# Linear attention and a maxout layer on one core: keys turned into one span over two PSUM banks, the 1e-9 of the queries as a sum of two, another order of the work

## The chip, the cores and the metric

The kernel runs on one core of a Trainium2 chip. The time is that of one execution on the device, in microseconds (us). The engines are PE (matrix products and transposes), DVE and ACT (element by element, from SBUF or PSUM), POOL (element by element, SBUF only) and the DMA queues, which the instruction streams of SP and ACT feed. Each engine works through its own list of instructions in order and waits on semaphores for the others.

## The reference

Attention without a softmax over pairs: queries are normalised over their 64 features, keys over the 576 positions, and the products of keys and values (64 by 64 for a head) are applied to the queries. The result goes through a layer of three products, the largest of which is kept, and an output product. All in float32, for 8 batches of 8 heads.

```python
q_s = np.exp(q - np.max(q, axis=-1, keepdims=True))
q_s = q_s / (np.sum(q_s, axis=-1, keepdims=True) + 1e-09)
k_s = np.exp(k - np.max(k, axis=2, keepdims=True))
k_s = k_s / (np.sum(k_s, axis=2, keepdims=True) + 1e-09)
kv = np.einsum('bhsd,bhse->bhde', k_s, v)
x = np.einsum('bhsd,bhde->bhse', q_s, kv)          # to 4608 rows of 512
h = np.maximum(np.maximum(x @ w1, x @ w2), x @ w3)  # 768 wide
out = h @ w_out
```

## The kernel before

Float32 products run as three products of a high and a low part in a faster type; each weight and each activation is split into such parts. The heads are taken in 32 pairs (a batch has four). The first two batches are "turned" pairs: `k_turned` (L623) transposes their keys on PE, so that positions lie along the free dimension, takes the maximum there on DVE, the exponential and its sum on ACT, and transposes back; `k_steps` (L695) goes on to the product with the values (L708), the reciprocal of the sum and the block matrix `bdf` (L720). The other 24 pairs are "plain": the maximum over positions is taken by POOL across partitions (L680), and two pairs at a time form a `Quad`, whose step on PE holds the products of keys and values of the next quad (L865) and the application to the queries of this one (L914). `q_steps` (L723) normalises the queries of a pair: maximum (L732 or L762), then, for pairs in `Q_BY_ACT`, one activation for each row with the maximum as bias and the sum as accumulator (L749, L767), else a subtraction, an exponential and a sum (L754 or L773, L778, L780); then the 1e-9 is added (L782), the reciprocal taken (L783) and multiplied in (L786).

The weights come in twelve slices (`Slice`, loaded at L489), are rounded and split on ACT, DVE and POOL (L505 to L548), and feed the gates: chunk by chunk for three chunks (`Chunk.gate`, L958, in groups of three products over one of four parts of x; L970 takes the maximum, L997 is the output product), and two chunks at a time with seven products instead of eight after that (`Duo.gates`, L1134, `Duo.second`, L1245).

The order of all this is not written down. Each part is a generator that yields steps, with an engine, a cost, what it waits for and which room (a PSUM bank, a buffer) it takes; `Streams.run` (L235) plays them against clocks of the engines and issues the instructions in the order that this gives. Ranks come from the tables at the head of the file, `LATE`, `Q_OFF`, `LOAD_OFF` and others. Where the planner sees PE idle, `fill` (L264) puts products of the identity with itself there (L457, from `filler`); ahead of the first step there are always eight, of a zeroed matrix (`IDLE_FIRST`). `FIRST_LOADS` gives the order of the first transfers (k, q, v: a pair's main rows; K, V: rest rows; w: a weight slice), and the first `FIRST_ON_ACT` of them may go to the queue of SP or of ACT. Eight semaphores are shared in turn by the transfers: a transfer that takes one again waits until the one that had it has landed.

PSUM has eight banks of 512 columns. Seven, `banks`, are handed out by the planner; the eighth is cut into four quarters (`small`, L452) for the small results: the last 64 columns of the turned keys (L635), their way back (L658), and the products of keys and values.

Of the kernel before, what the change touches and what calls it, by code (L numbers as in the profile page):

```python
# [36 lines left out]
SLICE = 225.18  # L37
LATE = (-245.5, -738.3, 170.7, 1076.1, 129.3, 336.8, 110.3, -591.5, 283.8, 139.9, -217.0, -419.4, 227.8, 729.6, 1717.3, 928.9, -4.1, 2054.6, 2040.9, 1513.5, 1739.1, 1826.7, 1494.9, 1573.0)
SUMS = (-733.7, -414.9, 85.3, 292.8, 1712.0, -374.3, 235.7, 406.3, 80.5)
KEPT = (107.0, -865.1, -45.2, -717.4, -1581.6, -900.1, -1174.0, -1366.7, -1728.2)  # L40
KEPT_RANK = 130.16
SLICE_OFF = (-340.2, -56.5, -907.2, -1080.6, -281.4, 597.2, 906.3, 417.9, 733.8, 516.7, 231.2, -111.0)
Q_OFF = (64.6, 1741.9, -395.6, -554.3, -297.6, 259.5, 483.6, 696.1, 858.9, 107.2, -846.4, 810.3, -294.1, 578.6, -714.3, -872.6, -323.0, 47.8, 428.2, 70.6, -145.8, 345.1, -642.9, 1226.8, 1104.8, -656.7, 635.3, 97.3, -96.9, 574.5, -54.6, -455.7)
LOAD_OFF = (-278.4, -22.2, -809.9, 466.9, 228.2, -747.5, -668.2, 212.2, -287.6, 241.8, -718.1, -298.3, 18.0, 918.3, -241.3, 259.7, -542.2, 133.3, -214.9, 1068.4, 1359.0, -703.2, 91.3, 840.3, 658.3, 313.8, 517.4, -68.2, 151.4, 996.4, 422.5, -604.7)
LOADS_AHEAD = 170.42

AT = (-454.7, 519.6, 1348.2, -133.6, 1086.9, 233.6, 436.9, 1101.5)
STEP = (-534.1, 491.2)
SLICES_AT = -84.14
SLICE_STEP = 134.98  # L50
SLICE_HI = -258.29
SLICE_LO = 126.09
GATES_AT = -85.68
FIRST_LOADS = 'kqKkwqvqvKqkvVwvVk'
FIRST_ON_ACT = 9
LEFT_AT = -132.76
# [10 lines left out]
SPARE_X, SPARE_KV, SPARE_RING, SPARE_LOAD, SPARE_KM = 2.52, 4.6, 0.0, 1.33, 1.58  # L67
# [245 lines left out]
def linear_attention_then_maxout_ffn(  # L313
# [48 lines left out]
    ps = ctx.enter_context(tc.tile_pool(name="ps", bufs=1, space=PSUM))  # L362
# [26 lines left out]
    bds = []  # L389
    early = early_stack.enter_context(tc.tile_pool(name="early", bufs=1))  # L390
# [6 lines left out]
    nc.vector.memset(ones, 1.0)  # L397
    count = early.tile([P, P], F32, name="count")
# [30 lines left out]
    def banks_of_heads(key):  # L429
        return (4, 5, 6) if key[-1] < NP * (PLAIN + 2) else range(7)  # L430
# [4 lines left out]
    for d in range((B + 1 - PLAIN) // 2):  # L435
# [3 lines left out]
        {"pf": banks_of_gates, "pa": banks_of_heads, "ring": RING, "ws": 1, "sums": 1, "halves": 2, "ps": 4, "keT": ROOM_KET, "hp": NJ, "tmp": N_TMP, "ke": 2, "qe": ROOM_QE, "qf": ROOM_QF, "qt": 2, "tb": N_TB, "qT": N_QT},  # L439
# [11 lines left out]
    quarters = ps.tile([P, 4, P], F32, name="ps")  # L451
    small = (quarters[:, i % 4, :] for i in itertools.count())  # L452
# [110 lines left out]
    class Pair:  # L563
# [131 lines left out]
        def k_steps(self):  # L695
# [18 lines left out]
            nc.vector.tensor_scalar(  # L714
                out=rk, in0=self.ks[:, 0:1], scalar1=self.ks[:, 1:2], scalar2=1e-9, op0=ALU.add, op1=ALU.add
            )
            nc.vector.reciprocal(out=rk, in_=rk)
# [845 lines left out]
```

## Time and profile before

| | |
|---|---|
| median of three runs | 659.4 us (653.69, 659.4, 660.97) |
| profiled execution | 657.82 us, its span 656.0 us |
| PE busy, of the span | 98% (clock 0.997 of full) |
| DVE, ACT, POOL busy | 69%, 43%, 9% |
| moved by DMA | 140.65 MB |

The page cuts the span into 40 slices of 16.4 us, each digit a tenth:

```profile
PE   9899999999999999899999999999999999999997
DVE  7998777679988988999989792144548614454521
ACT  5867485266563755743534454111113421112132
DMA  8899896368989899989999773466660536663012
```

PE has work nearly all the time; DVE and DMA are close to full over the first 23 slices (375 us), in which the attention is computed beside the gates, and half idle behind it. A busy PE includes the filler products.

### The profile page before, as it was taken

The numbers are of one execution on the slowest core, as the hardware profiler recorded it, in microseconds if no ns is written. First come the engines' busy times: TensorE is split into PE (matmuls) and PEld (weight loads), VectorE is DVE, ScalarE is ACT, GpSimd is POOL, SyncE is SP. The second block draws the span as 40 slices with busy tenths as digits, with TensorE's granted clock in tenths as the row PEclk, the third lists the DMA queues.
The fourth block names the chain that finished last, engine by engine and source line by source line (L and its number), as shares of the span: only waits on it lengthen the run. The fifth ranks groups of instructions, "written<-read, shape, count | busy, mean of one in ns | idle before, by whom it ended". The sixth has DMA issues, their size and how long they took to land.

```text
span 656.0 us, 10034 instructions
## 1 busy us (share of the span) xinstructions
PE 642.1 (98%) x3596; PEld 520.7 (79%) x3596; DVE 452.4 (69%) x785; ACT 281.4 (43%) x722; POOL 57.1 (9%) x71
## 2 busy tenths in 40 slices
PE   9899999999999999899999999999999999999997
PEld 8677778888777787677777887888888888888885
DVE  7998777679988988999989792144548614454521
ACT  5867485266563755743534454111113421112132
POOL 1322333201000010000110000000000000000000
PEclk9998999999999999999999999999999999999999
DMA  8899896368989899989999773466660536663012
GB/s 262 257 322 334 257 353 198 116 213 265 280 261 325 271 250 332 254 275 264 286 286 281 207 221 134 144 206 176 196 194 17 192 113 200 190 199 118 0 65 64
DMA packets 116770, 140.65 MB, mean 214 GB/s; under 512 B 53616, under 2 KB 75888, under 8 KB 115568
## 3 DMA queue, kind: packets, MB, share of 16 engines
q1 hardware_dynamic: 111552, 134.02, 66.8%
q10 hardware_dynamic: 5168, 6.00, 3.2%
q8 instruction: 28, 0.46, 0.3%
q14 instruction: 22, 0.18, 0.1%
HBM read 102.24 MB, written 37.75 MB: 213 GB/s over the span
## 4 chain that ended last, share of the span: by engine, by line
PE 84%; DMA 8%; DVE 2%; ACT 1%; SPq 1%; issue 0%; DVEq 0%; ACTq 0%
PE bank L1134 37%; PE bank L958 17%; PE bank L1245 15%; PE bank L997 7%; DMA kt<-in_k_dram 2%; DMA turned<-tb 2%; PE ps L865 2%; PE bank L457 1%; PE bank L914 1%; PE bank L831 1%; DMA wst<-in_moe_w_dram 1%; DMA qT<-turned 1%; DMA vt<-in_v_dram 1%; PE ps L708 1%; DMA qt<-in_q_dram 1%; PE bank L815 0%
## 5 line engine op out<-in xcount | busy, mean ns | idle before, releaser
L1134 PE MATMUL bank<-gw 128*128 128x512 f32 x1134 | 260.2, 390 | 0.5 <-DVE m L1202 0.5
L1134 PEld LDWEIGHTS bank<-gw 128*128 128x128 f32 x1134 | 212.3, 188 | 48.4 <-issue 1.6
L958 PE MATMUL bank<-gw 128*128 128x512 f32 x432 | 104.8, 399 | 0.0
L958 PEld LDWEIGHTS bank<-gw 128*128 128x128 f32 x432 | 81.1, 190 | 20.7 <-issue 3.9
L1245 PE MATMUL bank<-oh,halves 128*128 128x512 f32 x288 | 88.7, 389 | 0.0
L1245 PEld LDWEIGHTS bank<-oh,halves 128*128 128x128 f32 x288 | 54.1, 188 | 11.2
L1245 PE MATMUL bank<-ol,halves 128*128 128x512 f32 x144 | 56.3, 391 | 0.0
L958 PE MATMUL bank<-x,gw 128*128 128x512 f32 x216 | 49.9, 390 | 0.0
L958 PEld LDWEIGHTS bank<-x,gw 128*128 128x128 f32 x216 | 40.4, 188 | 9.2 <-issue 0.8
L1223 DVE TENSOR_TENSOR halves<-hf,halves 128x768 fp32r<-128x768 f32 (+2 forms) x30 | 23.6, 794 | 34.3 <-ACT halves L1221 34.2
L767 ACT ACTIVATE qt<-qt,qm 128x64 f32<-128x64 f32 x126 | 42.3, 339 | 11.6 <-DVE qm L762 9.8
L997 PE MATMUL bank<-oh,h 128*128 128x512 f32 x144 | 44.4, 389 | 0.0
L680 POOL PARTITION_ALL_REDUCE kma<-kh x24 | 18.3, 762 | 204.9 <-DVE kh L677 80.2
L1264 ACT COPY m<-bank 128x512 f32<-128x512 f32 x23 | 13.5, 589 | 52.4 <-PE bank L1245 52.4
L1196 ACT COPY m<-bank 128x512 f32<-128x512 f32 x18 | 10.6, 588 | 57.9 <-PE bank L1134 55.2
L1191 ACT COPY m<-bank 128x512 f32<-128x512 f32 x18 | 10.6, 587 | 54.8 <-PE bank L1134 50.0
L1245 PEld LDWEIGHTS bank<-ol,halves 128*128 128x128 f32 x144 | 27.0, 188 | 7.2 <-ACT left L923 0.8
L970 DVE TENSOR_TENSOR m<-bank,m 128x512 f32<-128x512 f32 x36 | 24.7, 685 | 11.2 <-PE bank L958 8.6
L997 PEld LDWEIGHTS bank<-oh,h 128*128 128x128 f32 x144 | 27.0, 188 | 5.6
L791 DVE STREAM_TRANSPOSE tb<-qt 128x576 f32<-128x576 f32 x24 | 30.3, 1269 | 0.2
L1198 DVE TENSOR_TENSOR m<-bank,m 128x512 f32<-128x512 f32 x18 | 12.4, 690 | 25.6 <-PE bank L1134 25.2
L997 PE MATMUL bank<-ol,h 128*128 128x512 f32 x72 | 28.3, 393 | 0.0
(162 smaller groups left out, 867.1 us busy)
## 6 DMA issues: line engine op xcount, KB each, us to landing
gw<-scratch SPq DMA_DIRECT2D x75, 512.0 KB, 3.7
gw<-scratch SPq DMA_DIRECT2D x39, 256.0 KB, 3.8
wst<-in_moe_w_dram SPq DMA_DIRECT2D x9, 1024.0 KB, 8.0
scratch<-bench SPq DMA_DIRECT2D x9, 1024.0 KB, 6.0
out_dram<-m SPq DMA_DIRECT2D x32, 256.0 KB, 2.2
vt<-in_v_dram SPq DMA_DIRECT2D x56, 128.0 KB, 5.2
scratch<-gw SPq DMA_DIRECT2D x27, 256.0 KB, 3.5
qt<-in_q_dram SPq DMA_DIRECT2D x24, 288.0 KB, 4.4
```

The source lines that it names most:

```text
L680: nc.gpsimd.partition_all_reduce(kma, kmv.rearrange("p h d -> p (h d)"), P, bass_isa.ReduceOp.max)
L767: nc.scalar.activation(out=rows3[:, i, :], in_=rows3[:, i, :], func=AF.Exp, bias=qm[:, i : i + 1], accum_out=qs[:, i : i + 1],)
L791: nc.vector.transpose(out=tb.rearrange("p e (c s) -> p s e c", s=QS), in_=self.qt.rearrange("p s (c e) -> p s e c", e=2))
L865: nc.tensor.matmul(out=kv[u][r, :NV], lhsT=p.ke[:, s, u, :], rhs=p.vt[:, u, s, :], start=(s == 0), stop=(s == 4))
L958: nc.tensor.matmul(out=ps, lhsT=l[:, cc], rhs=r, start=(cc == 0 and t == 0), stop=(cc == NC - 1 and t == 2))
L970: nc.vector.tensor_max(out=m, in0=self.m.pop((j, i)), in1=m)
L997: nc.tensor.matmul(out=po, lhsT=l, rhs=r[:, j, :], start=(j == 0 and i == 0), stop=(j == NJ - 1 and i == 2))
L1134: nc.tensor.matmul(out=po, lhsT=w[:, a, cc], rhs=x[:, b, cc], start=(first and cc == 0 and t == 0), stop=(cc == 1 and t == 2), skip_group_ ...
L1198: nc.vector.tensor_sub(out=ma, in0=po("w"), in1=ma)
L1223: nc.vector.tensor_sub(out=hl, in0=src, in1=hh.bitcast(F32))
L1245: nc.tensor.matmul(out=po, lhsT=l, rhs=r[:, j, :], start=(j == 0 and i == 0), stop=(end and i == 2))
L1264: nc.scalar.copy(out=o, in_=po)
```

## The change

The seventh bank and the eighth become one tile, `span`, of 1024 columns. The turned keys of a pair take its first 576 columns, always there, so that one maximum and one activation read all of them, across the border of the two banks; the other three quarters of the eighth bank stay for the small results. The sum of a pair's keys is then one number, and the 1e-9 is added from a column that holds it. For the queries a tile of sums has two places for each row: one is set to 1e-9 once, the other takes the sum, and a reduction over the two replaces the addition. The tables that order the work are all new (a line or two are shown), the first chunk's gates have four banks instead of five, and 24 pairs are in `Q_BY_ACT` instead of 18.

```diff
-FIRST_LOADS = 'kqKkwqvqvKqkvVwvVk'
-FIRST_ON_ACT = 9
+FIRST_LOADS = 'vvqwKkkvkVqqKVwqvk'
+FIRST_ON_ACT = 7
-Q_BY_ACT = (1, 2, 6, 7, 8, 9, 10, 11, 12, 13, 14, 17, 18, 20, 22, 25, 27, 31)
+Q_BY_ACT = (1, 3, 4, 5, 6, 9, 10, 11, 12, 13, 17, 18, 19, 20, 21, 23, 24, 25, 26, 27, 28, 29, 30, 31)
-FIRST_BANKS = 5
+FIRST_BANKS = 4
...
-    banks = [pf.tile([P, CH], F32, name=f"bank{i}") for i in range(7)]
+    banks = [pf.tile([P, CH], F32, name=f"bank{i}") for i in range(6)]
+    span = pf.tile([P, 2 * CH], F32, name="span")
+    banks.append(span[:, :CH])
...
+    sum_all = att.tile([P, 4, QS, 2], F32, name="qs", bufs=1)
+    sums_of = (sum_all[:, i % 4] for i in itertools.count())
...
+    nc.vector.memset(least, 1e-9)
+    nc.gpsimd.memset(sum_all, 1e-9)
...
-            yield Step("V", dve_reduce(CH) + dve_reduce(LEFT) + 0.13)
-            km = att.tile([P, 2], F32, name="km2", bufs=4)
-            nc.vector.tensor_reduce(out=km[:, 0:1], in_=kT, op=ALU.max, axis=AX.X, negate=True)
-            nc.vector.tensor_reduce(out=km[:, 1:2], in_=kTl[:, :LEFT], op=ALU.max, axis=AX.X, negate=True)
-            nc.vector.tensor_scalar(
-                out=km[:, 0:1], in0=km[:, 0:1], scalar1=km[:, 1:2], scalar2=None, op0=ALU.min
-            )
-            yield Step("A", act(CH) + act(LEFT) + 0.2, free=rooms)
+            yield Step("V", 0.75)
+            km = att.tile([P, 1], F32, name="km2", bufs=4)
+            nc.vector.tensor_reduce(out=km, in_=kT, op=ALU.max, axis=AX.X, negate=True)
+            yield Step("A", 0.98, free=rooms)
...
-            nc.scalar.activation(out=keT[:, :CH], in_=kT, func=AF.Exp, bias=km[:, 0:1], accum_out=ks[:, 0:1])
-            nc.scalar.activation(
-                out=keT[:, CH:], in_=kTl[:, :LEFT], func=AF.Exp, bias=km[:, 0:1], accum_out=ks[:, 1:2]
-            )
+            nc.scalar.activation(out=keT, in_=kT, func=AF.Exp, bias=km, accum_out=ks)
...
             yield Step("V", 0.34)
-            nc.vector.tensor_scalar_add(out=qs, in0=qs, scalar1=1e-9)
-            nc.vector.reciprocal(out=qs, in_=qs)
+            nc.vector.tensor_reduce(out=qr, in_=sums, op=ALU.add, axis=AX.X)
+            nc.vector.reciprocal(out=qr, in_=qr)
```

ACT's list at the start of the program, before (k, q, v are the first batch's tiles, wst a weight slice; in brackets the semaphores waited for, DMAHW those of transfers):

```order
L1387 DMA k_98<-in_k_dram 128x4x64
L1394 DMA k_98<-in_k_dram 64x2x64
L1387 DMA k_98<-in_k_dram 128x4x64
L1390 DMA q_99<-in_q_dram 128x2x256
L1398 ACT_TABLE_LOAD
L1398 ACTIVATE warm<-ones 128x1 [waits DVE_49]
L778 ACTIVATE qe<-qe 128x512 [waits DVE_49]
```

and now:

```order
L1392 DMA v_98<-in_v_dram 128x2x256
L497 DMA wst<-in_moe_w_dram 128x4x512
L1400 ACT_TABLE_LOAD
L1400 ACTIVATE warm<-ones 128x1 [waits DVE_49]
L1389 DMA k_96<-in_k_dram 128x4x64 [waits DMAHW2_49]
L1389 DMA k_96<-in_k_dram 128x4x64 [waits DMAHW4_49]
L778 ACTIVATE qe<-qe 128x512 [waits DVE_49]
L542 ACTIVATE wst<-wst 128x1024
```

The key loads have moved behind values and the first weight slice, and the first of the two waits on DMAHW2. DVE's list shows whose semaphore that is: its first operation on the weight slice waits on the same one.

```order
L782 TENSOR_REDUCE qr_142<-qs 128x8 [waits DVE_49]
L783 RECIPROCAL qr_142<-qr_142 128x8 [waits DVE_49]
L515 TENSOR_SCALAR left<-wst 128x1024 [waits DMAHW2_49]
L786 TENSOR_TENSOR qe<-qe,qr_142 128x512 [waits DVE_49]
L517 TENSOR_SCALAR left<-left 128x1024 [waits DVE_49]
```

The addition of the 1e-9 has become the reduction in the first of these rows. PE's list at the start, before:

```order
L457 MATMUL bank_81<-bdf_108 128x128 x8
L630 MATMUL bank_85<-ident,k_98 128x128 x4
L457 MATMUL bank_81<-ident 128x128 x7
L636 MATMUL ps<-ident,k_98 128x64
L457 MATMUL bank_81<-ident 128x128 x12
L657 MATMUL bank_86<-ident,keT 128x128 x4
L659 MATMUL ps<-ident,keT 64x128
L815 MATMUL bank_87<-ident,qe 128x128 x4
L457 MATMUL bank_81<-ident 128x128 x13
```

and now:

```order
L465 MATMUL bank_78<-bdf_106 128x128 x8
L638 MATMUL span<-ident,k_96 128x128 x4
L465 MATMUL bank_78<-ident 128x128 x7
L644 MATMUL span<-ident,k_96 128x64
L815 MATMUL bank_82<-ident,qe 128x128 x4
L465 MATMUL bank_78<-ident 128x128 x9
L658 MATMUL bank_83<-ident,keT 128x128 x4
L660 MATMUL span<-ident,keT 64x128
L465 MATMUL bank_78<-ident 128x128 x4
```

The fillers (L457, now L465) are fewer behind the first key's transposes, and the queries' transposes stand ahead of the way back of the keys. In all the list holds 74 filler products where it held 93: 66 for 71 up to the first long run of gates, 8 for 22 behind it. Behind that run PE's list was

```order
L457 MATMUL bank_83<-ident 128x128 x2
L708 MATMUL ps<-vt_94,ke 64x64 x10
L457 MATMUL bank_83<-ident 128x128 x4
L958 MATMUL bank_83<-gw 128x512 x12
L657 MATMUL bank_85<-ident,keT 128x128 x4
L659 MATMUL ps<-ident,keT 64x128
L815 MATMUL bank_87<-ident,qe 128x128 x4
```

and is now

```order
L658 MATMUL span<-ident,keT 128x128 x4
L660 MATMUL span<-ident,keT 64x128
L815 MATMUL bank_82<-ident,qe 128x128 x4
L465 MATMUL bank_81<-ident 128x128 x4
L638 MATMUL span<-ident,kt_88 128x128 x4
L644 MATMUL span<-ident,kt_88 128x64
L958 MATMUL bank_81<-gw 128x512 x3
```

One pair's turned keys are left behind the run, where there were three. Of the later batches, the groups of key and value products (L865) stood behind 378, 441, 516, 615, 675 and 741 of the gate and output products and stand now behind 393, 447, 510, 561, 657 and 720. On ACT 45 more single-row activations of queries stand in the later batches; POOL does three of the multiplications by the reciprocal (L786), and DVE copies six of the tiles of keys back from PSUM (L666, now L667) where it copied two.

More of the change, by code (lines that the diff above doesn't have):

```diff
@@ L35 @@
 EAGER = 0.3
[L37 to L42, printed above, removed]
@@ L429, in banks_of_heads @@
     def banks_of_heads(key):
+        if key[0] == "kT":
+            return (6,)
         return (4, 5, 6) if key[-1] < NP * (PLAIN + 2) else range(7)
@@ L438, in linear_attention_then_maxout_ffn @@
     st = Streams(
-        {"pf": banks_of_gates, "pa": banks_of_heads, "ring": RING, "ws": 1, "sums": 1, "halves": 2, "ps": 4, "keT": ROOM_KET, "hp": NJ, "tmp": N_TMP, "ke": 2, "qe": ROOM_QE, "qf": ROOM_QF, "qt": 2, "tb": N_TB, "qT": N_QT},
+        {"pf": banks_of_gates, "pa": banks_of_heads, "ring": RING, "ws": 1, "sums": 1, "halves": 2, "ps": 3, "kTl": 1, "keT": ROOM_KET, "hp": NJ, "tmp": N_TMP, "ke": 2, "qe": ROOM_QE, "qf": ROOM_QF, "qt": 2, "tb": N_TB, "qT": N_QT},
         {
@@ L449, in linear_attention_then_maxout_ffn @@
     late_pools, turn_pools, raws = [], [], []
-    quarters = ps.tile([P, 4, P], F32, name="ps")
-    small = (quarters[:, i % 4, :] for i in itertools.count())
+    quarters = span[:, CH:].rearrange("p (i n) -> p i n", i=4)
+    small = (quarters[:, 1 + i % 3, :] for i in itertools.count())
     def filler(i, n, t):
@@ L625, in k_turned @@
             n, kt = self.n, self.kt
-            rooms = [("pa", ("kT", n)), ("ps", ("kTl", n))]
+            rooms = [("pa", ("kT", n)), ("kTl", n)]
             yield Step("T", 0.74, [("k", n)], take=rooms + [("keT", n)], gives=("ksub", n))
-            kT = banks[st.bank("pa", ("kT", n))]
+            kT = span[:, :S]
             for s in range(4):
@@ L713, in k_steps @@
             rk = att.tile([P, 1], F32, name="rk", bufs=4)
-            nc.vector.tensor_scalar(
-                out=rk, in0=self.ks[:, 0:1], scalar1=self.ks[:, 1:2], scalar2=1e-9, op0=ALU.add, op1=ALU.add
-            )
+            nc.vector.tensor_scalar(out=rk, in0=self.ks, scalar1=least, scalar2=None, op0=ALU.add)
             nc.vector.reciprocal(out=rk, in_=rk)
@@ L742, in q_steps @@
                 rows3 = qe.rearrange("p s h d -> p (s h) d")
-                sums = qs.rearrange("p (s h) -> p s h", h=2)
                 if by_act:
@@ L1280, in left_queries @@
             nc.sync.dma_start(out=rows[r], in_=left_rows(q, b, slice(0, H)))
-        qm, qs = (att.tile([P, n], F32, name=name, bufs=4) for name in ("qm8", "qs8"))
+        qm = att.tile([P, n], F32, name="qm8", bufs=3)
+        qr = att.tile([P, n], F32, name="qr8", bufs=2)
         yield Step("V", dve_reduce(CH))
@@ L1288, in left_queries @@
         yield Step("V", dve_reduce(CH))
-        nc.vector.tensor_reduce(out=qs, in_=rows, op=ALU.add, axis=AX.X)
+        sums = next(sums_of)[:, :n]
+        nc.vector.tensor_reduce(out=sums[:, :, 0], in_=rows, op=ALU.add, axis=AX.X)
         yield Step("V", 0.34)
-        nc.vector.tensor_scalar_add(out=qs, in0=qs, scalar1=1e-9)
-        nc.vector.reciprocal(out=qs, in_=qs)
+        nc.vector.tensor_reduce(out=qr, in_=sums, op=ALU.add, axis=AX.X)
+        nc.vector.reciprocal(out=qr, in_=qr)
         yield Step("V", dve(CH), port="V")
-        nc.vector.tensor_tensor(out=rows, in0=rows, in1=qs.unsqueeze(2).broadcast_to([P, n, D]), op=ALU.mult)
+        nc.vector.tensor_tensor(out=rows, in0=rows, in1=qr.unsqueeze(2).broadcast_to([P, n, D]), op=ALU.mult)
         yield Step("T", 0.7, take=[("pa", ("lq", n - 1))], free=[("tmp", "ql")])
```

52 lines of the change are left out of this document (30 added, 22 removed).

## The prediction

> **What bounds the kernel now.** I read the page's busy shares first, then PE by stages, then what ended PE's waits, then the first 62 us of PE, DVE, ACT and the DMA queues in order of time.
>
> ```profile
> span 656.0 us, 10034 instructions
> ...
> PE 642.1 (98%) x3596; PEld 520.7 (79%) x3596; DVE 452.4 (69%) x785; ACT 281.4 (43%) x722; POOL 57.1 (9%) x71
> ...
> L457 PE MATMUL bank<-ident 128*128 128x128 f32 x170 | 22.9, 284 | 0.0
> ...
> L457 PE MATMUL bank<-bdf 128*128 128x128 f32 x16 | 3.5, 410 | 1.0 <-POOL bdf L410 1.0
> ```
>
> PE is busy 642.1 of 656.0 us, but 22.9 + 3.5 = 26.4 us of that are the filler products of line 457, which the planner puts where it expects PE to idle. What has to be computed is therefore 642.1 - 26.4 = 615.7 us, and no part of the change alters it: every product and transpose stays. The time can move only in the other 656.0 - 615.7 = 40.3 us: 26.4 of fillers and 13.9 of idle time. By stages (from and to in us, length, PE's busy time and instructions, granted clock, DMA share, GB/s):
>
> ```profile
> 0.00:4.70 4.70, 3.54 (x16) 1.00 0.50 115
> ...
> 4.70:21.60 16.90, 13.88 (x128) 1.00 1.03 316
> ...
> 21.60:42.20 20.60, 20.50 (x165) 1.00 0.91 262
> ...
> 42.20:99.10 56.90, 54.73 (x335) 0.97 0.97 320
> ...
> 250.00:316.00 66.00, 62.95 (x409) 1.00 0.98 279
> ...
> 600.00:656.00 56.00, 51.58 (x228) 1.00 0.13 40
> ```
>
> The idle time is 1.2 us at the start, 3.0 up to 21.6, 0.1, 2.2 up to 99.1, 3.05 between 250 and 316, and 4.4 in the tail. All fillers lie before 99.1 us. So the change is decided in the first 100 us, and 3 us more are to be had around 265 us. What holds PE there:
>
> ```profile
> 0.98 3.54 PE L457 MATMUL bank<-bdf 128*128 128x128 f32 x16 [0.98 <-POOL bdf L410]
> ...
> 4.74 0.65 PE L630 MATMUL bank<-ident,k 128*128 128x128 f32 x4 [0.23 <-DVE ident L405]
> ...
> 19.26 0.95 PE L708 MATMUL ps<-v,ke 128*64 128x64 f32 x20 [2.71 <-ACT keT L650]
> ...
> 264.70 0.76 PE L865 MATMUL ps<-vt,ke 128*64 128x65 f32 x16 [2.37 <-DMA vt<-in_v_dram]
> ```
>
> The first keys were there by 4.74 us (PE waited for the identity, not for them). After that PE waits for the chain of a key pair, through DVE and ACT, and around 265 us for a load of values.
>
> **The change, part by part.** *Keys over two banks.* Eight pairs lose one maximum and the minimum of two numbers on DVE, and one activation with its accumulator read on ACT:
>
> ```profile
> L641 DVE TENSOR_REDUCE km<-bank 128x1 f32<-128x512 f32 x8 | 5.3, 668 | 0.0
> ...
> L642 DVE TENSOR_REDUCE km<-ps 128x1 f32<-128x64 f32 x8 | 1.7, 212 | 0.0
> ...
> L643 DVE TENSOR_SCALAR km<-km 128x1 f32<-128x1 f32 x8 | 1.7, 215 | 0.3
> ...
> L649 ACT ACTIVATE keT<-bank,km 128x512 f32<-128x512 f32 x8 | 5.5, 688 | 0.9 <-DVE rk L714 0.5 <-DVE km L643 0.4
> ...
> L650 ACT ACTIVATE keT<-ps,km 128x64 f32<-128x64 f32 x8 | 2.5, 309 | 0.0
> ```
>
> Between 64 and 512 columns a maximum costs (668 - 212)/448 = 1.02 ns a column, so one over 576 should take 0.73 us; 0.36 us a pair, 2.9 us in all, go from DVE. An activation costs 0.85 ns a column: 0.74 us for 576, and with one accumulator read of 0.2 us less, some 0.45 us a pair go from ACT. No row reads across two banks: it can be as cheap as 512 columns (0.67) or as dear as both parts (0.88 and 1.00); I take the slope. PE waits for both at once in the chain of a pair.
>
> *The 1e-9.* A scalar add of eight numbers becomes a reduction of eight pairs of numbers. The add is dearer than its size:
>
> ```profile
> L782 DVE TENSOR_SCALAR qs<-qs 128x8 f32<-128x8 f32 x8 | 5.0, 627 | 0.5 <-ACT qe L749 0.4
> ...
> L782 DVE TENSOR_SCALAR qs<-qs 128x9 f32<-128x9 f32 x24 | 4.0, 167 | 0.0
> ...
> 29.28 1.21 DVE L782 TENSOR_SCALAR qs<-qs 128x8 f32<-128x8 f32 x1
> ...
> 27.93 2.54 POOL L529 TENSOR_TENSOR m<-left,wst 128x512 int32<-128x512 int32 x2 [1.21 <-ACT qe L778]
> ```
>
> Eight columns in the first stage take 627 ns, nine later take 167: the slow ones stand inside a POOL addition. A reduction of 64 columns shows no such spread (212 ns), so I take 0.17 us: 8 x 0.46 = 3.7 us go from DVE before 100 us (0 if the reduction is held up too). The accumulators are now written at every second place; I cost that at nothing, since they are read out one number at a time, and if it costs something ACT's idle time covers it (ACT is busy 281.4 of 656.0 us). One more memset on POOL stands ahead of those that the first fillers wait for; PE's wait there was 0.98 us for the constants and the first of eight, so it costs 0.1 us or so and is lost in the rest.
>
> *The first loads.* This is the dear part. ACT's queue now holds values, the first weights, and then two key loads that wait on a semaphore that is the first weights' own (DVE's first weight operation waits on the same one). The same kind of wait is seen before:
>
> ```profile
> 1.43 0.65 ACTq L1394 DMA_DIRECT2D k<-in_k_dram  x1
> ...
> 2.91 0.76 SPq L489 DMA_DIRECT2D wst<-in_moe_w_dram  x1
> ...
> 7.59 3.33 SPq L1387 DMA_DIRECT2D k<-in_k_dram  x2
> ...
> 10.96 1.39 SPq L1390 DMA_DIRECT2D v<-in_v_dram  x1
> ...
> 10.92 0.69 DVE L507 TENSOR_SCALAR left<-wst 128x1024 uint32<-128x1024 uint32 x1 [1.11 <-DMA wst<-in_moe_w_dram]
> ...
> wst<-in_moe_w_dram SPq DMA_DIRECT2D x8, 1024.0 KB, 8.0
> ...
> k<-in_k_dram SPq DMA_DIRECT2D x6, 128.0 KB, 6.2
> ...
> k<-in_k_dram ACTq DMA_DIRECT2D x2, 128.0 KB, 3.5
> ```
>
> Values on SP were issued at 10.96, as the first weights landed (DVE began at 10.92). In the change the first weights are issued about where L1394 stood, at 1.43. They land 8.0 us later, at 9.4, or no earlier than before, at 10.9, since as many bytes lie ahead of them; I take 10.2. Then half of the first pair's keys is issued and lands 3.5 to 6.2 us later, at 12.9 to 17.1; I take 14.5, nearer the short one, as ACT's queue is empty then. Behind these two issues (1.3 us) waits ACT's first exponential, and behind that DVE. PE's first transposes move from 4.74 to 14.5: **+9.8 us** (+8.2 to +12.4), not covered, since only the 8 filler products (16 passes) stand ahead of them.
>
> *Fillers.* The order holds 74 filler products for 93, each two passes in the trace: 38 passes fewer of 22.9/170 = 0.135 us: **-5.1 us**. Up to PE's first long run of gates 71 become 66; behind it 22 become 8.
>
> *Waits up to 42 us.* 3.0 + 0.1 by the stages, 2.71 of them at 19.26 for a pair's exponential. DVE's first weight operation moves from 10.92 to about 13 (ACT's exponential at 10.2 + 1.3, then sum and normalising), but DVE has 2.9 + 3.7 = 6.6 us less to do after that and a pair's chain is 0.8 us shorter, while PE, which starts late, has transposes and fillers behind each pair. I take the waits as gone, **-3.1 us**, with 0 as the other end. Waits from 42 to 99 (2.2 us): kept, by the same chain, 0 to 3.
>
> *Queries on ACT, 24 pairs for 18.* Five pairs of the later batches give up a sum and a subtraction of 576 columns on DVE, so some 5 x 1.5 = 7.5 us; ACT takes 45 activations more:
>
> ```profile
> L780 DVE TENSOR_REDUCE qs<-qt 128x9 f32<-128x576 f32 x10 | 7.5, 747 | 1.1 <-ACT qt L778 1.1
> ...
> L767 ACT ACTIVATE qt<-qt,qm 128x64 f32<-128x64 f32 x126 | 42.3, 339 | 11.6 <-DVE qm L762 9.8 <-DMA qT<-turned 1.6
> ```
>
> These pairs lie behind 99 us, where PE waits 3.05 us in all: hidden behind the gates' products, a gain of at most those 3.05 us, and a loss only if ACT, less than half busy, became late. Three multiplications go from DVE to POOL and two pairs' copies from ACT to DVE: about as much, hidden in the 6.6 us above, and a wait of a few tenths on PE if it is not.
>
> *The later order.* Key and value groups of line 865 stand closer: from the third to the fourth 51 gate products for 99, and the fourth comes 54 products earlier in the program. I keep the 3.05 us.
>
> Sum: 9.8 - 5.1 - 3.1 = +1.6 us. The profiled execution took 657.8 us (1.8 around its span); **659.4 us**. The median of the three runs is 659.4, but they spread from 653.7 to 661.0, so I measure against the profiled one: +0.2%, no change by the 1% that a measurement of this kernel can tell.
>
> [...] The first passes took 421 ns where later ones took 275, and PE then never stood still for over 2.71 us:
>
> ```profile
> L457 PE MATMUL bank<-ident x170: 272/275/422, 5.2 to 98.8; 128*128 128x128 f32 x170
> ...
> L457 PE MATMUL bank<-bdf x16: 274/421/583, 1.0 to 4.2; 128*128 128x128 f32 x16
> ```
>
> If a wait of ten microseconds makes PE slow again, a restart like the first one follows: 16 passes in 3.54 us against 16 x 0.135 = 2.2, so +1.4 us, and up to twice that as the passes are sparse. The time would be 660.8 to 662. [...]
>
> **The rivals.** *Slower, 0.15:* the fourth group stalls. Its place is 54 products earlier, 12.3 us at 6.05/26 = 0.23 us each, between groups 14 us apart.
>
> ```profile
> 204.65 6.05 PE L958 MATMUL bank<-gw 128*128 128x512 f32 x26
> ...
> 211.95 0.27 PE L914 MATMUL ps<-qT,bd 64*64 64x64 f32 x2
> ...
> 202.64 0.68 SPq L803 DMA_DIRECT2D qT<-turned  x1
> ...
> qT<-turned SPq DMA_DIRECT2D x16, 288.0 KB, 5.1
> ...
> 200.00:260.00 60.00, 60.00 (x399) 47.46 (x398) 52.20 (x99) 32.26 (x99) 4.57 (x6) 1.00 0.97 296
> ```
>
> The turned queries were read at 202.6 and landed at 207.7, 4.2 us ahead of their use. If loads and DVE do not come forward by more than 4.2 of the 12.3 us, PE stalls up to 8.1: 667.5. For it speaks a DMA share of 0.97; against it DVE's 7.5 us less in a stage where it is 52.20 of 60 us busy. *Faster, 0.18:* the keys land at the early end (-1.6), the values' waits at 265 (-3.05) and those from 42 to 99 (-2.2) go: 652.5; were the keys not held by the weights and there by 8 us (6.2 us behind an issue near 2), 652.9 by that alone. Against it stands the semaphore. *PE slow after its wait, 0.15:* 661. *It does not do what it says:* a reduction held up by POOL like the add gives back 3.7 us of DVE, in part to PE: 661 to 663, and counts with the forecast's 0.52.
>
> **How the numbers follow.** Forecast 0.52 at 659.4, its own range 654 to 664 by the ends of the waits and of the keys' landing. With the slow clock (0.15) and half of each outer rival the range 651 to 668 leaves out less than 2 in 10. Faster by over 1% (below 651.2) needs all of the faster rival and some of the unknown: 0.12. Slower (above 664.4) is the fourth group's stall and a part of the late keys: 0.17. Within: 0.71.
>
> **What would show it.** Right: PE idle from about 4.7 to 13 - 17 us until a key load; ACT's first exponential at 11 to 13; a 576-column maximum at 0.70 to 0.76 us; sums of two at 0.15 to 0.2 us with no outliers; 132 filler passes in 17 to 18 us. Wrong: keys transposed before 10 us; new idle time at line 865 of over 4 us; more than 4 us of waits between 20 and 99 us, which would say that DVE, not the filler count, sets that stretch.

## The result and the profile after

The changed kernel takes 665.1 us in the median of four runs (664.76 to 667.09), where the kernel before takes 658.6 (653.69 to 660.97): a ratio of 1.0103, 95% interval 1.0069 to 1.0137. It is slower, by about one per cent. Run once more beside other kernels it came to 1.0126 (1.0097 to 1.0156). One execution of all that follow, of the kernel a_best, took 856.6 us at a granted clock of 0.75 and is left out of its ratio. The profiled execution took 664.76 us, its span 663.0, against 657.82 and 656.0 before: 7.0 us more span.

The busy shares of the page first, and the rows of the filler products:

```profile
span 663.0 us, 10035 instructions
...
PE 640.3 (97%) x3558; PEld 516.8 (78%) x3558; DVE 441.6 (67%) x760; ACT 290.4 (44%) x803; POOL 60.9 (9%) x73
...
L465 PE MATMUL bank<-ident 128*128 128x128 f32 x132 | 19.3, 293 | 0.0
...
L465 PE MATMUL bank<-bdf 128*128 128x128 f32 x16 | 3.8, 431 | 1.1 <-POOL bdf L416 1.1
```

PE is busy 1.8 us less than before and idle 22.7 us for 13.9. DVE has lost 10.8 us of work and ACT has gained 9.0, and neither shows in the time. Where PE idles now, by stages (from and to, length, PE's busy time and instructions, granted clock, DMA share, GB/s):

```profile
4.70:21.60 16.90, 9.81 (x80) 0.80 1.01 294
21.60:42.20 20.60, 18.28 (x160) 1.00 0.83 230
42.20:99.10 56.90, 53.94 (x337) 1.00 0.94 296
...
200.00:250.00 50.00, 48.40 (x345) 1.00 1.00 301
250.00:316.00 66.00, 64.01 (x368) 1.00 0.95 282
316.00:400.00 84.00, 83.43 (x498) 1.00 0.87 250
400.00:500.00 100.00, 99.35 (x493) 1.00 0.56 173
```

Idle time rose by 4.1 us between 4.7 and 21.6, by 2.2 up to 42.2, by 0.8 up to 99.1 and by 1.6 between 200 and 250, fell by 1.1 up to 316, and rose by 1.2 in 316 to 500, where there had been none. The first line also carries a clock of 0.80. What ended PE's waits (in all, times, longest):

```profile
PE span L638 <- DMA k<-in_k_dram: 7.1, 1, 7.1
PE span L638 <- ACT ke L667: 2.0, 3, 1.1
PE span L865 <- DMA vt<-in_v_dram: 1.6, 1, 1.6
PE bank L997 <- ACT h L973: 1.6, 1, 1.6
PE span L709 <- DVE km L649: 1.5, 3, 0.9
...
PE span L638 <- DVE ke L667: 1.0, 1, 1.0
PE span L1134 <- DVE rks L882: 0.7, 2, 0.4
PE span L1245 <- DVE rks L882: 0.7, 1, 0.7
```

Two kinds of wait are new. One is for the first keys, 7.1 us. The other has `span` on both sides: transposes of the next pair's keys (L638) wait for the copy of the last pair's (L667), 3.0 us, and gates and output products (L1134, L1245) wait for the reading of the keys' sums (L882), 1.4 us. Before, no transpose of keys waited for more than 0.3 us on a copy, and no gate on L882.

The first wait in order of time, on ACT, its queue and PE:

```profile
1.28 0.48 ACTq L497 DMA_DIRECT2D wst<-in_moe_w_dram  x1
...
8.28 1.36 ACTq L1389 DMA_DIRECT2D k<-in_k_dram  x2
9.68 0.63 ACT L778 ACTIVATE qe<-qe 128x512 f32<-128x512 f32 x1 [6.39 <-issue]
...
11.94 1.09 PE L638 MATMUL span<-ident,k 128*128 128x128 f32 x4 [7.09 <-DMA k<-in_k_dram]
12.82 2.99 PE L465 MATMUL bank<-ident 128*128 128x128 f32 x14
...
16.44 2.17 PE L465 MATMUL bank<-ident 128*128 128x128 f32 x18
...
13.00:14.00 1.00, 1.00 (x7) 0.50 1.10 303
16.00:17.00 1.00, 1.00 (x11) 1.00 1.07 382
```

The key loads were issued when the first weights had landed, 7.0 us behind their issue; ACT's first exponential waited behind them for 6.4 us. Behind the wait PE ran at half its clock until 15.5 us: 14 filler passes took 2.99 us, where 18 took 2.17 just after.

The two mechanisms themselves did what was said of them:

```profile
L649 DVE TENSOR_REDUCE km<-span 128x1 f32<-128x576 f32 x8 | 6.0, 752 | 4.4 <-PE span L644 3.0 <-PE span L709 1.4
...
L782 DVE TENSOR_REDUCE qr<-qs 128x8 f32<-128x16 f32 x8 | 1.3, 159 | 0.0
...
L653 ACT ACTIVATE keT<-span,km 128x576 f32<-128x576 f32 x8 | 5.9, 736 | 2.9 <-PE span L709 1.9 <-DVE km L649 1.0
```

A maximum over 576 columns in two banks takes 752 ns and the activation 736, on the slope of the old rows; the sum of two takes 159 ns for 627. But in the first row DVE waits 1.4 us, and in the last ACT waits 1.9 us, for products of keys and values (L709) that the maximum and the activation do not read.

### The profile page after: what moved, and what is told of

Same layout as the page of the kernel before. It is cut to its first block, busy times and chain, and to the rows that moved or that the text cites. A ratio compares the mean times of both kernels' runs of the same rounds, so it can differ in the third digit from the quotient of the medians.

```text
span 663.0 us, 10035 instructions
## 1 busy us (share of the span) xinstructions
PE 640.3 (97%) x3558; PEld 516.8 (78%) x3558; DVE 441.6 (67%) x760; ACT 290.4 (44%) x803; POOL 60.9 (9%) x73
## 4 chain that ended last, share of the span: by engine, by line
PE 82%; DMA 8%; DVE 5%; ACT 3%; issue 1%; ACTq 0%; DVEq 0%
PE bank L1134 31%; PE bank L958 14%; PE bank L1245 12%; PE span L1134 8%; PE bank L997 7%; DMA wst<-in_moe_w_dram 3%; PE span L1245 3%; PE span L865 2%; DMA vt<-in_v_dram 2%; DMA turned<-tb 2%; PE bank L914 1%; PE bank L465 1%; PE span L709 1%; DMA gw<-scratch 1%; PE span L638 1%
## 5 line engine op out<-in xcount | busy, mean ns | idle before, releaser
L1134 PE MATMUL bank<-gw 128*128 128x512 f32 x912 | 215.3, 390 | 0.3 <-DMA gw<-scratch 0.3
L1134 PEld LDWEIGHTS bank<-gw 128*128 128x128 f32 x912 | 170.8, 188 | 39.4 <-issue 3.2
L958 PE MATMUL bank<-gw 128*128 128x512 f32 x432 | 103.3, 395 | 0.0
L958 PEld LDWEIGHTS bank<-gw 128*128 128x128 f32 x432 | 80.2, 188 | 19.4 <-issue 3.1
L1245 PE MATMUL bank<-oh,halves 128*128 128x512 f32 x240 | 73.9, 389 | 0.0
L767 ACT ACTIVATE qt<-qt,qm 128x64 f32<-128x64 f32 x171 | 57.2, 339 | 12.0 <-DVE qm L762 7.9
L1134 PE MATMUL span<-gw 128*128 128x512 f32 x222 | 57.1, 391 | 0.7 <-DVE rks L882 0.7
L1245 PEld LDWEIGHTS bank<-oh,halves 128*128 128x128 f32 x240 | 45.1, 188 | 9.3
L1134 PEld LDWEIGHTS span<-gw 128*128 128x128 f32 x222 | 41.4, 188 | 10.5 <-DVE rks L882 1.6
L1245 PE MATMUL bank<-ol,halves 128*128 128x512 f32 x120 | 46.8, 390 | 0.0
L767 ACT ACTIVATION_READ_ACCUMULATOR qt<-qt,qm 128x1 f32 x171 | 32.6, 191 | 0.0
L1264 ACT COPY m<-bank 128x512 f32<-128x512 f32 x19 | 11.2, 588 | 42.6 <-PE bank L1245 42.6
L970 DVE TENSOR_TENSOR m<-bank,m 128x512 f32<-128x512 f32 x36 | 24.6, 685 | 6.8 <-PE bank L958 6.3
L1196 ACT COPY m<-bank 128x512 f32<-128x512 f32 x15 | 8.8, 588 | 44.8 <-PE bank L1134 42.1
```

The costliest lines, as they stand in the source:

```text
L767: nc.scalar.activation(out=rows3[:, i, :], in_=rows3[:, i, :], func=AF.Exp, bias=qm[:, i : i + 1], accum_out=sums[:, i, 0:1],)
L958: nc.tensor.matmul(out=ps, lhsT=l[:, cc], rhs=r, start=(cc == 0 and t == 0), stop=(cc == NC - 1 and t == 2))
L970: nc.vector.tensor_max(out=m, in0=self.m.pop((j, i)), in1=m)
L1134: nc.tensor.matmul(out=po, lhsT=w[:, a, cc], rhs=x[:, b, cc], start=(first and cc == 0 and t == 0), stop=(cc == 1 and t == 2), skip_group_ ...
L1196: nc.scalar.copy(out=ma, in_=po("x"))
L1245: nc.tensor.matmul(out=po, lhsT=l, rhs=r[:, j, :], start=(j == 0 and i == 0), stop=(end and i == 2))
```

## The experiments

All ratios are to the kernel before on the same chip, with 95% intervals; the median of before was 658.8 to 660.1 us in these sessions. The sessions were on more than one chip, and the change itself stands at 1.0103 in one and at 1.0126 in another. From the widths of the intervals, the difference of two ratios is uncertain by 0.4 to 0.5%: a_two, a_keys and a_best are clear of the change by that, a_late, a_swap, a_warm and a_warm_h are not.

| kernel | what | ratio | interval |
|---|---|---|---|
| the change | | 1.0103 | 1.0069 to 1.0137 |
| after_again | the same | 1.0126 | 1.0097 to 1.0156 |
| a_two | changed order, keys in two tiles | 1.0050 | 1.0028 to 1.0072 |
| a_late | two tiles only behind the turned pairs | 1.0073 | 1.0043 to 1.0102 |
| a_swap | key half and weight slice exchanged | 1.0083 | 1.0052 to 1.0114 |
| a_warm | 34 fillers ahead for 8 | 1.0091 | 1.0062 to 1.0120 |
| a_warm_h | the same, a read behind the rounding | 1.0082 | 1.0049 to 1.0114 |
| a_keys | keys first in the loads | 1.0037 | 1.0010 to 1.0064 |
| a_best | a_two, a_keys and the read together | 1.0003 | 0.9972 to 1.0034 |
| a_keys_h | a_keys, a_late and the read together | 1.0029 | 1.0005 to 1.0052 |
| b_sum | before, 1e-9 as a sum of two | 0.9995 | 0.9974 to 1.0017 |
| b_fill | the same, ten more fillers | 1.0022 | 1.0001 to 1.0043 |
| b_merge | both mechanisms, tables of before | 1.0169 | 1.0137 to 1.0201 |
| b_merge_two | the same order, keys in two tiles | 1.0142 | 1.0084 to 1.0200 |
| b_merge_late | the same, two tiles behind the turned pairs | 1.0127 | 1.0069 to 1.0185 |

The second row is the changed kernel as it is:

> The changed kernel once more, unchanged, on the same chip as these, for a tighter interval and a second profile. Both theories: 664 to 666, ratio 1.008 to 1.012; PE waits 7 us for the keys and runs at half its clock for 3 to 4 us behind that wait in this execution too.

Measured: 667.2 us, a little above what was expected. Its profile has the same two marks: a wait of 6.9 us ahead of the transposes of the first keys (it names a load of queries as what ended last), and 14 filler passes in some 3.0 us behind it. In the kernels named a_ the tables and the places of all instructions are those of the change, but for the edit; b_sum and b_fill have the places of before.

### The tile over two banks

```diff
-    banks = [pf.tile([P, CH], F32, name=f"bank{i}") for i in range(6)]
-    span = pf.tile([P, 2 * CH], F32, name="span")
-    banks.append(span[:, :CH])
+    banks = [pf.tile([P, CH], F32, name=f"bank{i}") for i in range(7)]
+    quarters = pf.tile([P, 4, P], F32, name="ps")
...
-            kT = span[:, :S]
+            kT = banks[6]
...
-            kTl = kT[:, CH:]
+            kTl = quarters[:, 0, :LEFT]
```

and the two maxima, the minimum and the two activations of before.

> The changed kernel with the keys of a pair in two tiles again, as before: 512 columns in the seventh bank, 64 in a quarter of the eighth, two maxima and two activations. Every engine's order stays that of the changed kernel. Theory A: the one tile over two banks makes each write or read of it wait for the last use of any part of it, so the transposes of the next pair wait for the copy of the last one (3.0 us on PE), and gates in the seventh bank wait for the sums of keys (1.4 us); the time falls by 3 to 4.4 us from 665.1, to 660.7 to 662.1, though DVE has 2.9 us and ACT 3.6 us more to do. Theory B: these waits only stand where others would stand, and the cost lies in the first loads and the order; the time stays at 665 or rises to 667.

Measured: 661.8 us, ratio 1.0050, so some 3.5 us less (3.3 by the medians). Theory A, though DVE and ACT have more to do. The second pair's transposes in the order, with the semaphores they wait for, in the changed kernel and in this one:

```
L638 MATMUL span<-ident,k_96 128x128 [waits DMAHW6_49,DMAHW4_49,DVE_49]
L636 MATMUL bank_84<-ident,k_97 128x128 [waits DMAHW6_49,DMAHW4_49]
```

In the built program the value of DVE's semaphore in the first row is that of the copy of the last pair's 64 columns out of the eighth bank (L667), though the transpose writes the seventh; and the second pair's maximum waits for a signal of PE that the last product of L709 gives, into another quarter. In the traces the copy ends at 19.96 us and the transposes begin at 20.02; with two tiles they begin at 20.42, while the copy lasts until 20.50. The dependencies are drawn for the tile, so one tile over two banks joins what two tiles kept apart. With two tiles the transpose of the 64 columns (L642, eighth bank) still waits for the copy, 0.30 us at 26.44 and 0.54 at 33.01, and the four of the seventh bank do so no more at those pairs. Whether the waits that are left within the eighth bank are needed was not shown. Not all of the 3.0 us comes from joining the two banks: the wait of 1.07 us at 75.49 in the changed kernel is there with two tiles too (1.25 at 74.52), since at that pair the way back of the last keys was in the seventh bank itself.

Where the 3 to 4 us lie is told by the same groups of products of keys and values in order of time, first the changed kernel, then a_two:

```profile
298.49 1.39 PE L865 MATMUL span<-vt,ke 128*64 128x65 f32 x40
...
302.99 0.96 PE L1134 MATMUL span<-gw 128*128 128x512 f32 x3 [0.39 <-DVE rks L882]
...
350.86 1.39 PE L865 MATMUL span<-vt,ke 128*64 128x65 f32 x40
...
360.75 0.96 PE L1134 MATMUL span<-gw 128*128 128x512 f32 x3 [0.32 <-DVE rks L882]
...
403.28 0.92 PE L865 MATMUL span<-vt,ke 128*64 128x65 f32 x24
```

```profile
296.95 1.39 PE L870 MATMUL ps<-vt,ke 128*64 128x65 f32 x40
...
348.57 1.39 PE L870 MATMUL ps<-vt,ke 128*64 128x65 f32 x40
...
399.55 1.39 PE L870 MATMUL ps<-vt,ke 128*64 128x65 f32 x40
```

The distance is 1.5 us at the first, 2.3 at the second, 3.7 at the third, and 4.6 at the end of PE (658.5 and 653.9). Two thirds of it arise behind 298 us, where nobody looks for the keys of the first batches: the quarters and the gates' seventh bank are still one tile. These are single executions, and in them a wait cost more than its idle time: from the group at 298 us to the next one (316.19 and 313.93) the changed kernel takes 0.7 us longer, for one wait of 0.39.

```diff
+        span_stack.close()
+        pool = ctx.enter_context(tc.tile_pool(name="parted", bufs=1, space=PSUM, reuse_waits="tile"))
+        banks[6] = pool.tile([P, CH], F32, name="bank6")
+        quarters.append(pool.tile([P, 4, P], F32, name="ps"))
```

> The changed kernel; only once the last turned pair is done, the two-bank tile is given up and its banks become two tiles again, one for gates and one for the quarters. The order is the same on every engine. Theory A: of what two tiles from the start won (3.3 us), the later waits are the larger part: gates and output products in the seventh bank no longer wait for the reads of sums of keys (0.7 us up to 320 us, 1.4 up to 403, 0.9 behind it by the distance of the same groups); the time falls by 2 to 3 us, to 662.1 to 663.1. Theory B: the waits of the first pairs' transposes for the copies carry it, and the time stays within 1 us of 665.1.

Measured: 662.6 us, ratio 1.0073, 2.0 us less by the ratios. In its profile PE's waits for the sums of keys are gone, and between 400 and 500 us it is never idle. Theory A by the profile; by the time alone, with intervals that overlap with that of the change, it would be open.

### The first loads

```diff
             if ch == "w":
-                slices[g].load(start, N_ST, N_X, queue(e))
+                if g == 0:
+                    nc.scalar.dma_start(out=k0[:, 0:4, 1, :], in_=head_rows(k, 0, 1))
...
-                    queue(e).dma_start(out=k0[:, 0:4, h, :], in_=head_rows(k, 0, h))
+                    if h == 1:
+                        slices[0].load(start, N_ST, N_X, queue(e))
```

> The changed kernel with two transfers exchanged: the second half of the first pair's keys is issued where the first weight slice was (1.3 us), and the slice where that half was, behind its semaphore. All else stays in place. Theory A: the keys' late landing and the slow clock behind it cost 5 to 7 us; PE's first transposes move from 11.9 to about 7 us, the clock stays at 1.00 or recovers, and the time falls to 658.5 to 660.5, with the slice 4 us later at no cost. Theory B: the chain of the first pairs through the weights on DVE sets this stretch; the wait comes back before 30 us and the time stays within 1.5 us of 665.1.

Measured: 663.3 us, ratio 1.0083: 1.8 us less by the medians, between the theories, but by the ratios 1.3 us, which is theory B; the intervals overlap. The transposes began at 10.59 us, not at 7. The half that was moved was issued at 1.27 and landed 4.4 us later. The other half was on SP's queue as before, issued at 2.5 us in both kernels; in the changed one it landed 6.1 us later, in this one 7.9, each time within 0.4 us behind the weights' megabyte on ACT's queue. That megabyte was not 4 us later, as had been expected, but 0.7: it was issued at 2.01 for 1.28. A small load on SP's queue, the keys' rest, issued at 1.73 in both, tells what held it. In the changed kernel, and then in this one (KB, us from issue to landing):

```profile
wst<-in_moe_w_dram ACTq DMA_DIRECT2D x1, 1024.0 KB, 7.0
...
k<-in_k_dram SPq DMA_DIRECT2D x1, 32.0 KB, 6.5
```

```profile
wst<-in_moe_w_dram ACTq DMA_DIRECT2D x1, 1024.0 KB, 8.3
...
k<-in_k_dram SPq DMA_DIRECT2D x1, 32.0 KB, 4.3
```

Issued behind the megabyte it took 6.5 us, ahead of it 4.3, with the same loads ahead of it on its own queue. So the semaphore was not the whole of it: the loads that were issued behind the megabyte landed with it (the keys' rest at 8.2 us in the changed kernel, the megabyte at 8.3) or up to 0.4 us behind it (the half of the keys), though they were on the other queue.

```diff
+FIRST_CARRIED = 'h0 h1 q0 K0 w0 v0 v1'
...
-                filler(0, 7, 1.0)
+                filler(0, 24, 1.0)
```

Here the first seven places, each on its queue as planned, carry the two halves of the keys, queries, the keys' rest, the weight slice and the values; 17 more filler products stand behind the first transposes, and no run has one without the other.

> The changed kernel with the first seven places of the loads carrying other tiles: both halves of the first pair's keys first, then queries, key rest, first weight slice, values; no load waits on the slice's semaphore, so ACT isn't held. 24 filler products for 7 stand behind the first four transposes, to keep PE busy until the queries come. Else the same order. Theory A: the first transposes start near 5 us and the first product with the values at 16 to 17.5 us for 20.8; what PE gains there (3 to 4.5 us) stays, and the time falls to 660.6 to 662. Theory B: the gain is taken back around 269 us, where ACT's queue waits for a transfer and PE for ACT, as in the kernel with 34 fillers, where 1.6 us of gain at 19 us were 0 at 286 us; the time falls by at most 1.5 us.

Measured: 661.8 us, ratio 1.0037, 4.3 us less than the ratio of the change. Theory A. The profile shows the start and one more wait (times of PE):

```profile
4.44 0.65 PE L639 MATMUL span<-ident,k 128*128 128x128 f32 x4
...
17.60 0.91 PE L639 MATMUL span<-ident,k 128*128 128x128 f32 x4 [2.54 <-DVE ke L668]
...
20.20 4.21 PE L466 MATMUL bank<-ident 128*128 128x128 f32 x18
...
22.00:23.00 1.00, 1.00 (x7) 0.50 0.56 125
25.00:26.00 1.00, 1.00 (x4) 1.00 0.83 223
```

The keys were transposed at 4.44, but the second pair's transposes waited 2.54 us for the copy, through the shared tile, and PE was then at half its clock until 24.7 us: 18 filler passes took 4.21 us. The last group at 403.3 began at 401.2, so 2 us were left there in this execution.

### The slow clock

```diff
-IDLE_LEAST, IDLE_KEPT, IDLE_SHARE, IDLE_FIRST, IDLE_LAST = 0.35, 0.1, 0.85, 8, 110.0
+IDLE_LEAST, IDLE_KEPT, IDLE_SHARE, IDLE_FIRST, IDLE_LAST = 0.35, 0.1, 0.85, 34, 110.0
```

> The changed kernel with 34 filler products ahead of the first step for 8, so that PE is busy over its 7.1 us wait for the keys; nothing else differs. Theory A: the wait makes PE slow for 3.8 us after it; with PE kept busy the granted clock stays 1.00 from 5 us on, and the time falls by 1.3 to 2 us, to 663.1 to 663.8. Theory B: the slow passes are hidden behind the chain of the first pair: the clock is 1.00 and the time stays at 665.

Measured: 664.1 us, ratio 1.0091: the interval holds the ratio of the change, so the time cannot tell. The profile can: PE had the full clock behind the wait, and the first product of keys and values (L709) came at 19.25 us for 20.81. These 1.6 us were 0.8 at the first later group (156.0 for 156.8) and gone behind 273 us, where PE waited 3.0 us for ACT's rounding of a maximum (L973) where the changed kernel waits 1.6. The longer wait is not what took the gain: at its end this kernel was still 1.0 us ahead (268.43 for 269.45). But behind it the clock was at half, from 270.0 to 273.4 us, and the twelve products from there to the next group took 4.6 us (to 273.02) for 3.2 (to 272.67). In this execution the slow clock that was spared at 12 us came back at 270. What held ACT, in the changed kernel:

```profile
262.94 0.35 ACTq L795 DMA_DIRECT2D turned<-tb  x1
268.12 0.62 ACTq L803 DMA_DIRECT2D qT<-turned  x1
268.78 0.62 ACT L973 CAST h<-m 128x512 fp32r<-128x512 f32 x1 [6.32 <-DMA turned<-tb]
```

ACT's queue writes turned queries to memory and reads them back at once; the read waits for the write to land, here until 5.2 us behind the write's issue, and the rounding that PE needs stands behind the read.

```diff
+            if n == HELD_BACK:
+                held.append(read)
...
             nc.scalar.copy(out=h, in_=m)
+            while held:
+                held.pop()()
```

with `HELD_BACK = 19`, the pair whose read it is.

> The kernel with 34 filler products ahead, in which one transfer on ACT's queue, the read of the turned queries of pair 19, is issued behind the next rounding of a maximum (line 973) and no longer ahead of it. Theory A: that read held ACT for 8.9 us around 263 us and PE for 3.0 us; without it the 1.6 us won at the start come through and 1.6 us more, and the time is 661 to 662.3 for 664.1. Theory B: another transfer is as late there (the queues are over 0.9 busy from 200 to 316 us); PE waits 2 us or more nearby for it and the time stays at 663.5 or above.

Measured: 663.6 us, ratio 1.0082, inside the interval without it. In its profile that wait is gone, but this execution (659.0) was the lowest of twelve, so it cannot stand for them. By the time theory B holds; whether the read costs anything stays open.

The same question in the order of before, on b_sum, ahead of the products of line 708:

```diff
+            if n == 0:
+                filler(0, 10, 1.0)
```

> The kernel before with the 1e-9 as a sum of two and ten more filler products ahead of the first pair's product with the values, where PE waits 2.7 to 3.5 us for the exponential and was at half its clock for 3.5 us behind it in one profile (21.5 to 25 us). Theory A: with PE busy there the clock stays full, and the time falls by 0.8 to 1.7 us, to 656.6 to 657.5 for 658.3, with less spread. Theory B: the slow passes only fill a later wait for the same chain: 658 to 658.8.

Measured: 660.7 us, ratio 1.0022. This is above both ranges, so theory A fell: the clock was 1.00 up to 42.2 us, and in the profile PE waited 4.2 us for values at 266.8 where it had waited 1.7. From 264.6 to 271.4 us the clock was at half. The group at 266.83 is 2.7 us behind that of b_sum (264.10), the next one 4.5 (294.75 for 290.28). In this execution what was won at the start was not kept at 265 us, where a transfer ended the wait of 4.2 us and the clock was at half.

### The 1e-9, and the parts together

In the kernel before, this alone, with the tile of sums that it needs:

```diff
-            nc.vector.tensor_scalar_add(out=qs, in0=qs, scalar1=1e-9)
+            nc.vector.tensor_reduce(out=qr, in_=sums, op=ALU.add, axis=AX.X)
```

> The kernel before with one part of the change, the 1e-9 of the queries as a reduction over two places; the order is that of before on every engine. Theory A: the eight sums of the first batches take 0.16 us for 0.63, DVE gives up 3.7 us before 100 us, and of PE's 5.3 us of waits there 0 to 1.5 go: 657 to 658.6. Theory B: reading one number in two and writing accumulators at every second place costs ACT or DVE something: 659 to 661.

Measured: 658.3 us, ratio 0.9995. The eight sums took 166 ns each in the profile, and the time did not move: DVE's 3.7 us are off the path, and the stride of two costs nothing that can be measured.

The edits of a_two, a_keys and the read of pair 19 behind the rounding, in one kernel:

> The changed order with keys in two tiles, the first loads with the keys ahead, and the read of pair 19 behind the rounding. Theory A: the three causes add up (3.3, 3 to 4.5 and 1.6 us): 655.5 to 657.5, below the kernel before. Theory B: what is won early is lost at loads of values or turned queries between 200 and 316 us, where the transfers are over 0.9 busy: 659.5 to 661.5, no better than the kernel before.

Measured: 658.8 us, ratio 1.0003: between the two ranges, and no better than the kernel before, as theory B has it. PE waits 2.8 us for turned queries between 222 and 271 us, where the changed kernel has no such wait. It takes back all that the change had lost, and no more: what else the new order does (fewer fillers, 24 pairs of queries on ACT) brings nothing that can be measured.

The same, but with the edit of a_late in place of that of a_two:

> The changed order with the keys ahead in the first loads, the read of pair 19 behind the rounding, and the keys over two banks kept, the tile given up once the turned pairs are done. Against the same with two tiles from the start (ratio 1.0003) it tells what the one maximum and one activation are worth while the turned pairs run. Theory A: the transposes' waits for the copies cost more than the shorter chain wins: 1 to 2 us above, 659.7 to 660.8. Theory B: the shorter chain wins: 657 to 658.7.

Measured: 661.0 us, ratio 1.0029: just above the range of theory A, with an interval that overlaps with that of a_best. While the turned pairs run PE waits 6.1 us for copies in this profile, where a_best has 2.0:

```profile
PE span L656 <- ACT ke L685: 3.4, 3, 2.4
PE span L656 <- DVE ke L685: 2.7, 2, 1.7
```

### The mechanisms under the tables of before

```diff
-FIRST_LOADS = 'vvqwKkkvkVqqKVwqvk'
-FIRST_ON_ACT = 7
+FIRST_LOADS = 'kqKkwqvqvKqkvVwvVk'
+FIRST_ON_ACT = 9
...
-FIRST_BANKS = 4
+FIRST_BANKS = 5
```

and all other tables so too.

> The changed kernel with the tables of before (ranks, first loads, 18 pairs of queries on ACT): the keys over two banks and the 1e-9 as a sum, in nearly the order of before; 93 filler products or a few less. Theory A: the tile that two banks share costs what two tiles won in the changed order, 3 us or so, and the keys come early as before: 660.5 to 662.5. Theory B: the two mechanisms are worth what they take from DVE and ACT (2.9 and 3.6 us, and 3.7 for the 1e-9), and only the new order costs: 656 to 658.5.

Measured: 670.2 us, ratio 1.0169, outside both. At the first later group it was 1.6 us behind the kernel before (151.6 for 150.0), at the last 13.6 (412.15 for 398.56). The turned keys' fixed bank is a new rule for the planner, and with the old ranks it made another order behind 150 us. Two more kernels kept that order:

> The kernel with the tables of before and both mechanisms (ratio 1.0169), with the keys in two tiles again; its order is kept on every engine. Theory A: most of its 11 us are the tile that two banks share: the ratio falls to 1.000 to 1.006 (659 to 663). Theory B: the planner, with another rule for banks, made an order that is worse by itself behind 150 us (its loads came late: 3.3 us of waits for weights, 1.4 for values): the ratio stays at 1.011 to 1.017 (666.5 to 670).

> The same kernel with the keys over two banks, the tile given up once the turned pairs are done. Theory A: the later waits in the shared tile carry most of the 11 us, since the distance to before is 1.6 us at 151 us and 13.5 at 412: the ratio falls to 1.002 to 1.008. Theory B: the order carries them: 1.012 to 1.017.

Measured: 667.4 and 667.7 us, ratios 1.0142 and 1.0127. Theory B: with two tiles again the kernel is still 1.4% slower, so most of the 1.7% is that order (PE waits 2.3 us for weights and 1.8 for a rounding on DVE that came late); the tile's own part, 0.3%, cannot be told from none by these intervals. So the price of the tile is shown in the changed order, and not in this one.

## Why the prediction was wrong

It named 659.4 us and no change; the time is 665.1, inside its range and slower by 1.0%, to which it gave 0.17. By its own steps, against the profiled execution, whose span grew by 7.0 us:

| step | forecast | measured |
|---|---|---|
| keys late | +9.8 | +6.9 (7.09 for 0.23) |
| fillers | -5.1 | -3.4 (23.0 for 26.5 of busy time) |
| waits up to 99 us | -3.1 | +0.1 |
| waits behind 99 us | 0 | +1.8 |
| other work of PE | 0 | +1.6 |

- **Keys late: right in kind.** PE idled until a key load, from 4.85 to 11.94; the first weights landed at 8.28 and not at 10.2, so the wait is 2.9 us shorter than taken. The reason given, the weights' semaphore, is a part of it: a_swap took it away and the keys came only 1.4 us earlier, because the other half, of which the prediction says nothing, then landed behind the weights' megabyte.
- **Waits: the step that failed.** "I take the waits as gone": 2.7 us went at 19 us, but 2.2 came up to 42.2 and 0.8 up to 99.1. The prediction's own sign of being wrong came true: PE idles 5.3 us from 21.6 to 99.1 (2.3 before), over the 4 us that it named. It would have put this down to DVE, but DVE did have less to do. With two tiles (a_two) the idle time up to 42.2 falls from 2.3 to 0.9 us, so there it was the tile; from 42.2 to 99.1 it stays (3.0 and 3.1), and that part is not explained. The prediction read the merged tile as a saving of instructions and never asked what else uses the two banks. a_two shows the price: 3.3 us, of which two thirds fall behind 298 us, where the prediction had put nothing.
- **Waits behind 99 us.** "I keep the 3.05 us" failed too: it became 4.8 (1.6, 2.0, 0.6 and 0.6). The rival of the fourth group had another place: that group ran on time, and the sixth, at 245 us, waited 1.6 us for values.
- **The slow clock: right as a rival.** Half the clock came with a wait of 7.1 us. It took 1.3 us more for 14 filler passes and 0.4 for the four transposes, 1.7 where the rival said 1.4. That it matters for the time was not shown: a_warm spared it here and met it again at 270 us. That a wait of ten microseconds makes PE slow was an assumption, which no row of the kernel before showed; the 1.4 us were estimated from its first passes. By the prediction PE stood still for no more than 2.71 us behind these, but it overlooked a row that it shows: the stage from 42.2 to 99.1 us has a clock of 0.97, so the time of the kernel before held a slow stretch already (see the last section).
- **Fillers.** The count was right (132 and 16 passes); 14 of them ran at half the clock.
- **Other work of PE.** Put at nothing, it grew by 1.6 us; 0.4 are the slow transposes, and the rest is not explained.
- **The 1e-9 and the maximum: right.** 159 ns without a slow one, 752 ns inside the 0.70 to 0.76 us named; neither moves the time, as b_sum shows for the first.

So the two causes that were shown are the late keys (a_keys, 0.66% by the two ratios, with its 17 filler products) and the shared tile (a_two, 0.53%). Undone together, with one read moved that showed no effect by itself, they give back the whole 1.0% (a_best).

## What to carry to other kernels

Before two banks become one tile to save an instruction, list everything that uses either bank, over the whole program, and price the waits that the tile joins: here the instructions saved were off the path, and most of the loss arose over 200 us behind the code that was changed. For the first transfers read the order of issue over all queues, not only the semaphore: a large load that was issued ahead of a tile on another queue delayed it nearly as much (with the semaphore's wait gone the first keys were still transposed only at 10.59 us, for 11.94 with it, where the kernel before had them at 4.74). And a gain ahead of a stretch where transfers end the waits has to be followed to its far side before it is counted: of the 1.6 us that a_warm had won at 19 us nothing was left behind 273.

## What the hardware showed

Half the clock came with waits of 7.1, 4.2, 3.5, 3.0 and 2.5 us (the change, b_fill, b_sum, a_warm, a_keys), but not behind the wait of 2.7 us at 19 us in the kernel before. In that same kernel it came at 62.1 us, where no wait since had been longer than 1.3:

```profile
60.80 0.95 PE L708 MATMUL ps<-vt,ke 128*64 128x64 f32 x20 [1.29 <-DVE km L642]
...
62.20:65.50 3.30, 3.30 (x12) 0.50 0.86 270
```

Nor does it come by a fixed lag: in b_sum the product right behind the wait of 3.5 us ran at full speed, and the slow stretch began 1.5 us later:

```profile
20.07 0.95 PE L711 MATMUL ps<-v,ke 128*64 128x64 f32 x20 [3.51 <-ACT keT L653]
...
21.60:24.00 2.40, 2.40 (x12) 0.50 0.80 216
```

Nor did a longer wait bring a longer slow stretch: 6.8 us at half the clock followed the wait of 2.54 us in a_keys, and 3.4 us, from 270.0 to 273.4, that of 3.0 us in a_warm. So no length of wait can be named from these runs as the one that costs the clock. Nor does the granted clock always show it: in a_swap it reads 1.00 from 11 to 16 us, while 14 filler passes behind a wait of 5.7 us took 2.81 us, as slow as in the change.
